# Forgetting attention with a channel mix on one core: the first two heads' bias summed in place, a 1e-9 added by another engine, and first sums of values put into a transpose bank

## The chip, the cores and the metric

The kernel is one program on one core of a Trainium2 chip. The metric is the device time of one execution in microseconds (us), taken as the median of several runs. Engines are named as in the profile: PE (matmul) with PEld (its weight load), DVE (vector), ACT (scalar), POOL (GpSimd) and SP, which issues every DMA of this kernel from one queue.

## The reference

Eight batches of eight heads with 576 positions and 64 features go through attention with a forgetting bias; the result, laid out as 512 features, goes through a gated channel mix.

```python
scores = (q @ k.T) / sqrt(D)
cum = cumsum(maximum(s, 0), axis=-1)
bias = -(cum[:, :, :, None] - cum[:, :, None, :])
scores = where(causal, -1e9, scores + minimum(bias, 0))
attn = exp(scores - max(scores))
attn = attn / (sum(attn) + 1e-9)
x = (attn @ v)                       # (batch, seq, 512)
x_prev = x one position earlier
xk = mu_k * x + (1 - mu_k) * x_prev
xr = mu_r * x + (1 - mu_r) * x_prev
out = sigmoid(xr @ w_r) * (maximum(xk @ w_k, 0) ** 2 @ w_v)
```

## The kernel before, in words

Every instruction is first a task in a list (`Plan.add`): its engine, an estimated duration, what it reads and writes, and a due time. `Plan.run` then plays the list forward through a model of the engines, computes new due times backward from what came out, and repeats that `PASSES` times; the order with the shortest modelled time is written out. So an engine executes its instructions in an order fixed by the estimates, and waits at the head of its queue if reality is later. The estimates belong to the edits: `dve` and `pool` give an instruction its modelled duration, and `dma` gives a transfer `land=700` ns after its issue, to which the model adds 1,000 ns after any DMA and 30 to 500 ns before its user. While PE has nothing planned at the start, the planner writes small matmuls into its queue (line 359) until the first product of weights and values, `plan.busy_from`.

The attention runs head by head in "visits" of two heads (`hp`), batch after batch. Batch 0 is visited in two parts: queries 0 to 319 (`A`, 320 keys) for all four pairs, then queries 320 to 575 (`Z`). The other seven batches are visited whole (`ALL`). That is 72 passes through `scores`: 8 of `A`, 8 of `Z`, 56 of `ALL`. The first eight visits (16 heads' passes) use values and weights in plain float32 (`plain`), the others split them in a high and a low part.

`scores` for one head: a row of prefix sums of `s` is read from DRAM (`cum_d`) broadcast on all 128 partitions as `CB` (tag `cb`, two buffers, line 605). POOL makes the causal copy `M` of its blocks at the diagonal (tag `mask`, two buffers, line 624). PE multiplies queries and keys into a PSUM bank (line 642 plain, 653 split), DVE adds the bias and keeps the row's extreme value (line 668), ACT takes the exponent and the row's sum (line 686, into `sums`), DVE adds 1e-9 (line 723) and takes the reciprocal (line 728, into `rinv`), and POOL multiplies the weights `W` by it (line 699).

The prefix sums come from `prefix_sums`: `s` of all 64 heads lands on 64 partitions (line 419), DVE clips and scales it (424) and scans it (431), and a DMA stores it to `cum_d` (437). Its two buffers have the tag `cb` too.

`weighted` for one head: PE transposes the normalized weights block by block into PSUM banks with the tag `t` (line 745; two such banks, taken in turn), ACT copies a block to `ph` (772, 804), DVE takes what `ph` lost into `pl` (776, 811). In an `ALL` pass four banks are filled so: the last one holds the blocks of keys 256 to 383 in columns 0 to 255, and of keys 384 to 511 in columns 256 to 383. Then PE multiplies by the values (line 861 plain, 877 split): the sums of queries 0 to 127 go into a fifth bank of the tag `t`, those of queries 128 to 575 into the bank `po`. ACT (898 plain, 905) and DVE (909) take them to `xT`, which is stored to `x_d` (line 1202).

The channel mix works on 18 chunks of 256 positions: `x` is loaded from `x_d` (line 1104), mixed (951, 960) and split (979, 983), PE does three matmul passes for each weight block (1012, 1054, 1079), and `g` is stored (1096). The weights arrive in float64 words and are converted once by ACT, DVE and POOL (lines 483 to 514). POOL also makes the low parts of keys (`KL`, line 582), queries (`G`, 593) and values (`V`, 538), for each head.

Of the kernel before, what the change touches and what calls it, by code (L numbers as in the profile page):

```python
# [15 lines left out]
AF = mybir.ActivationFunctionType  # L16
# [37 lines left out]
class Plan:  # L54
# [210 lines left out]
        return [-x for x in at]  # L265


    PASSES = 4

    def run(self):  # L270
        best = None
# [14 lines left out]
def forgetting_attention_then_channel_mix(  # L286
# [38 lines left out]
    def sbuf(shape, tag, bufs=1, dtype=F32):  # L325
        return plan.buffer(sb, shape, dtype, tag, bufs)

    def bank(n, tag, bufs=1):
        return plan.buffer(psum, [P, 512 * n], F32, tag, bufs)
# [7 lines left out]
    def pe(emit, reads, writes, n, m=P, cycle=1.0625 / 2.4, k=P):  # L337
        i = plan.add("PE", n * cycle, emit, reads, writes, land=0.83 * m + 1)
        plan.columns[i] = n * k / P * (4 if cycle > 1 else 1)
        return i  # L340

    def act(emit, reads, writes, n, extra=51, table=0):
        return plan.add("ACT", n * 0.8333 + extra, emit, reads, writes, land=table)

    def dve(emit, reads, writes, n, rate=0.96):
        return plan.add("DVE", n / rate + 68, emit, reads, writes)

    def pool(emit, reads, writes, n, extra, rate=0.8333):
        return plan.add("POOL", n * rate + extra, emit, reads, writes)

    def dma(emit, reads, writes, ns):
        return plan.add("SP", max(520, ns), emit, reads, writes, land=700)


    idle = bank(1, "po", 1)
# [56 lines left out]
    cum_d = fixed(dram.tile([B * H, S], F32, name="cum_d"))  # L412

    def prefix_sums():
        cum = sbuf([B * H, S], "cb", 2)
        spos = sbuf([B * H, S], "cb", 2)
        ones = sbuf([B * H, S], "raw", 4)
        dma(
            lambda: nc.sync.dma_start(spos.get(), s.rearrange("b h t -> (b h) t")),
            [], [spos], 410,  # L420
        )
        pool(lambda: nc.gpsimd.memset(ones.get(), 1.0), [], [ones], S, 36)
        dve(
            lambda: nc.vector.tensor_scalar(
                out=spos.get(), in0=spos.get(), scalar1=0.0, scalar2=ISCALE,
                op0=ALU.max, op1=ALU.mult,
            ),
            [], [spos], S,
        )
        dve(  # L430
            lambda: nc.vector.tensor_tensor_scan(
                out=cum.get(), data0=ones.get(), data1=spos.get(), initial=0.0,
                op0=ALU.mult, op1=ALU.add,
            ),
            [ones, spos], [cum], 2 * S,
        )
        dma(lambda: nc.sync.dma_start(cum_d.ap, cum.get()), [cum], [cum_d], 410)


    def load_mu():  # L440
# [78 lines left out]


    ALL, A, Z = tuple(range(NQ)), (0, 1, 2), (3, 4)

    def load_values(b, hp, nk, plain):

# [75 lines left out]
    def scores(b, h, tiles, G, KH, KL):  # L600

        NK = KN[tiles[-1]]
        CB = sbuf([P, NK], "cb", 2)
        dma(
            lambda: nc.sync.dma_start(
                CB.get(), cum_d.ap[b * H + h : b * H + h + 1, 0:NK].broadcast_to([P, NK])
            ),
# [108 lines left out]
        for t in tiles:  # L716
            m, n, W = QN[t], KN[t], pt[t]
            i = 0
            for k0, w in [(0, n)] if n <= 512 else [(0, n // 2), (n // 2, n // 2)]:
                i = products(t, m, i, k0, w, W)  # L720
            exponents(t, m, n, i - 1, W)
        dve(
            lambda: nc.vector.tensor_scalar(  # L723
                out=rs(rinv), in0=rs(sums), scalar1=1.0e-9, scalar2=None, op0=ALU.add
            ),
            [(sums, t) for t in tiles], [rinv], len(tiles),
        )
        dve(lambda: nc.vector.reciprocal(rs(rinv), rs(rinv)), [], [rinv], 8 * len(tiles))  # L728
        for t in tiles:
# [3 lines left out]
    def weighted(j, pt, V, xT, tiles, plain):  # L733
# [17 lines left out]
        def block(ps, at, kb, n=1):  # L751

            ts = [t for t in tiles if t > kb]
            q0, q1 = QS[ts[0]], QS[ts[-1]] + P
            m = q1 - q0
            for k in range(kb, kb + n):
                for t in ts:
                    turn(ps, at + (k - kb) * m + QS[t] - q0, t, k * P, P)

            def strips(x):  # L760
                a = col(kb, q0)
                if n == 1:
                    return x.get()[:, a : a + m]
                step = col(kb + 1, q0) - a
                return x.get()[:, a : a + n * step].rearrange("p (k x) -> p k x", x=step)[:, :, 0:m]

            def src():
                x = ps.get()[:, at : at + n * m]
                return x if n == 1 else x.rearrange("p (k x) -> p k x", x=m)

            ks = range(kb, kb + n)
            act(lambda: nc.scalar.copy(strips(ph), src()), [ps], [(ph, k) for k in ks], n * m)  # L772
            if plain:
                return
            dve(
                lambda: nc.vector.tensor_tensor(  # L776
                    out=strips(pl), in0=src(), in1=f32(strips(ph)), op=ALU.subtract
                ),
                [ps] + [(ph, k) for k in ks], [(pl, k) for k in ks], n * m,
            )  # L780
# [47 lines left out]
        if len(tiles) == NQ:  # L828
            ps = bank(1, "t", 2)
            halves(ps, 0, 1, NQ - 1)  # L830
            ps = bank(1, "t", 2)
            block(ps, 0, 0)
            ps = bank(1, "t", 2)
            halves(ps, 384, 0, 0)
            block(ps, 0, 1)
            ps = bank(1, "t", 2)
            block(ps, 0, 2)
            block(ps, 256, 3)
        elif tiles[0] == 0:
            ps = bank(1, "t", 2)  # L840
            halves(ps, 256, 0, 0)
            block(ps, 0, 0)
            ps = bank(1, "t", 2)
            halves(ps, 0, 1, 2)
            block(ps, 256, 1)
        else:
            ps = bank(1, "t", 2)
            block(ps, 0, 0, 2)
            ps = bank(1, "t", 2)
            block(ps, 0, 2)  # L850
            ps = bank(1, "t", 2)
            halves(ps, 0, 3, 4)
            block(ps, 256, 3)
        lo, ot = 64 * j, 64 * (1 - j)

        def values(po, base, kb, q0, m, x, first, last):
            parts = [("h", kb), "l" if kb == NQ - 1 else kb]
            if plain:
                r = slice(0, 64 if kb == NQ - 1 else P)
                i = pe(  # L860
                    lambda: nc.tensor.matmul(
                        po.get()[:, q0 - base : q0 - base + m],
                        V.get()[r, kb],
                        x.get()[r, col(kb, q0) : col(kb, q0) + m],
                        start=first,
                        stop=last,
                    ),
                    [V] + [(x, i) for i in parts[: 2 if kb < NQ - 1 else 1]],
                    [po], m, P, 4 / 2.4, r.stop,
                )  # L870
                if plan.busy_from is None:
                    plan.busy_from = i
                return

            both = x is ph or last
            pe(
                lambda: nc.tensor.matmul(  # L877
                    po.get()[: P if both else 64, q0 - base : q0 - base + m],
                    V.get()[:, kb, 2 * j : 2 * j + (2 if both else 1), :],
                    x.get()[:, col(kb, q0) : col(kb, q0) + m],  # L880
                    start=first,
                    stop=last,
                ),
                [(V, i) for i in range(3)] + [(x, i) for i in parts], [po], m, P if both else 64,
            )

        def sums(po, q0, q1):

            todo = []
            for kb in range(-(-q1 // P)):  # L890
                a = max(q0, kb * P)
                todo += [(kb, a, x) for x in ((ph, pl) if kb < NQ - 1 and not plain else (ph,))]
            for i, (kb, a, x) in enumerate(todo):
                values(po, q0, kb, a, q1 - a, x, i == 0, i == len(todo) - 1)
            n = q1 - q0
            if plain:
                act(
                    lambda: nc.scalar.copy(
                        xT.get()[lo : lo + 64, 1 + q0 : 1 + q1], po.get()[lo : lo + 64, :n]
                    ),  # L900
                    [po], [(xT, (j, q0))], n,
                )
                return
            act(
                lambda: nc.scalar.copy(xT.get()[lo : lo + 64, 1 + q0 : 1 + q1], po.get()[ot : ot + 64, :n]),
                [po], [(xT, (j, q0))], n,
            )
            dve(
                lambda: nc.vector.tensor_tensor(  # L909
                    out=xT.get()[lo : lo + 64, 1 + q0 : 1 + q1],  # L910
                    in0=po.get()[lo : lo + 64, :n],
                    in1=xT.get()[lo : lo + 64, 1 + q0 : 1 + q1],
                    op=ALU.add,
                ),
                [po], [(xT, (j, q0))], n,
            )

        for q0, q1 in sums_of(tiles):
            sums(bank(1, "t", 2) if q1 == P else bank(1, "po", 1), q0, q1)

    def sums_of(tiles):

# [234 lines left out]
        due += 2 * STEPS[x]  # L1157

    plan.due = -2.0e5
    prefix_sums()  # L1160
    QKs, Vs = {}, {}

# [115 lines left out]
```

## Time and profile before

| | |
|---|---|
| median of 3 runs | 927.6 us (923.38 to 927.82) |
| the profiled execution | 925.86 us, its span 923.9 us, 2.0 us lie outside the span |
| mean granted PE clock | 0.978 |
| busy shares of the span | PE 95%, PEld 81%, DVE 76%, ACT 74%, POOL 51% |
| DMA | 109.56 MB, mean 119 GB/s |

Busy time is the union of an engine's instructions. PE's matmuls are pipelined and their ends are modelled, so its share is an upper limit of its work. The first 100 us differ from the rest: the weights are loaded and converted there, 243 GB/s move, and the granted PE clock is lower.

### The profile page before, as it was taken

How to read it: one execution, taken by the hardware profiler on the slowest of the kernel's cores; microseconds unless marked ns; L12 is line 12 of the kernel's file. 1: busy time of each engine (PE TensorE's matmuls, PEld its weight loads, DVE VectorE, ACT ScalarE, POOL GpSimd, SP SyncE). 2: the span in 40 equal slices, each digit the busy share in tenths (PEclk: the TensorE clock that was granted, in tenths of full speed). 3: DMA queues.
4: the chain of work that ended last, by engine and by line, in shares of the span. 5: the costliest groups of instructions: out<-in, count | busy, mean ns of one | idle time of the engine just before them, and what ended most of it. 6: DMA issues, size and time to landing. Idle time of an engine off the chain costs nothing.

```text
span 923.9 us, 18424 instructions
## 1 busy us (share of the span) xinstructions
PE 882.2 (95%) x5540; PEld 751.4 (81%) x5540; DVE 701.7 (76%) x2455; ACT 683.1 (74%) x1809; POOL 474.0 (51%) x783
## 2 busy tenths in 40 slices
PE   6979899999999999999999999999999999999998
PEld 3558777877879798978888988888888879888886
DVE  7956889989987888678878787878787878545431
ACT  4868798989987888688868697878786867445331
POOL 4876697787774476555546654555564641100000
PEclk7779999999999999999999999999999999999999
DMA  7878545455452344434243533343434220101100
GB/s 255 256 224 234 150 148 151 131 155 152 123 168 91 110 130 117 120 108 143 90 137 105 151 104 115 95 132 99 144 103 126 79 85 15 41 31 36 46 23 23
DMA packets 63651, 109.56 MB, mean 119 GB/s; under 512 B 10176, under 2 KB 25024, under 8 KB 63552
## 3 DMA queue, kind: packets, MB, share of 16 engines
q1 hardware_dynamic: 63552, 108.40, 39.4%
q8 instruction: 43, 0.70, 0.3%
q14 instruction: 56, 0.46, 0.2%
HBM read 89.33 MB, written 19.04 MB: 117 GB/s over the span
## 4 chain that ended last, share of the span: by engine, by line
PE 33%; DVE 10%; ACT 7%; issue 2%; DMA 2%; POOL 0%; DVEq 0%; ACTq 0%; POOLq 0%
PE m L1012 12%; PE m L1079 8%; PE m L1054 5%; PE t L745 3%; PE po L877 3%; DVE W L668 3%; PE s L653 2%; DVE xp L960 2%; ACT xp L951 2%; ACT W L686 2%; DVE rinv L723 1%; DVE pl L776 1%; DMA x<-x_d 1%; DVE xT L909 1%; ACT ph L772 1%
## 5 line engine op out<-in xcount | busy, mean ns | idle before, releaser
L1012 PE MATMUL m<-xh,w_k 128*128 128x256 f32 x1152 | 232.6, 288 | 2.2 <-DVE kl L1041 2.1
L686 ACT ACTIVATE W<-W,nm 64x64 f32<-64x64 f32 (+4 forms) x320 | 179.7, 562 | 37.7 <-DVE nm L668 31.8
L745 PE MATMUL t<-ident,W 128*128 128x128 f32 (+1 forms) x960 | 191.4, 281 | 14.7 <-DVE pl L776 6.5
L1079 PE MATMUL m<-w_v,kh 128*128 128x512 f32 x576 | 201.3, 406 | 0.0
L1012 PEld LDWEIGHTS m<-xh,w_k 128*128 128x128 f32 x1152 | 186.2, 190 | 4.9 <-DVE kl L1041 2.9
L699 POOL TENSOR_SCALAR W<-W,rinv 64x64 f32<-64x64 f32 (+4 forms) x320 | 163.8, 531 | 42.7 <-DVE rinv L728 29.9
L1012 PE MATMUL m<-xl,w_k 128*128 128x256 f32 x576 | 165.1, 287 | 0.2
L745 PEld LDWEIGHTS t<-ident,W 128*128 128x128 f32 (+1 forms) x960 | 114.0, 132 | 53.3 <-DVE pl L776 13.8
L582 POOL TENSOR_TENSOR KL<-raw,KH 128x576 fp32r<-128x576 f32 x64 | 92.1, 1438 | 110.7 <-ACT KH L578 101.0
L1079 PEld LDWEIGHTS m<-w_v,kh 128*128 128x128 f32 x576 | 107.2, 189 | 18.0 <-ACT g L1066 0.2
L653 PE MATMUL s<-KH,G 128*64 128x64 f32 (+3 forms) x360 | 112.9, 321 | 4.5 <-DVE nm L668 3.9
L1079 PE MATMUL m<-w_v,kl 128*128 128x512 f32 x288 | 116.6, 405 | 0.0
L960 DVE SCALAR_TENSOR_TENSOR xp<-x,mu,xp 128x256 f32<-128x256 f32 (+3 forms) x192 | 80.6, 420 | 47.3 <-ACT xp L951 44.7
L668 DVE CUSTOM_DVE_ANT_0 W<-s,cb 128x64 f32<-128x64 f32 (+3 forms) x256 | 94.5, 374 | 26.4 <-PE s L653 19.3
L776 DVE TENSOR_TENSOR pl<-t,ph 128x512 fp32r<-128x512 f32 x224 | 105.2, 481 | 10.1 <-ACT ph L772 8.8
L1012 PEld LDWEIGHTS m<-xl,w_k 128*128 128x128 f32 x576 | 109.4, 190 | 1.7 <-DVE xl L983 0.9
L653 PE MATMUL s<-KL,G 128*64 128x64 f32 (+3 forms) x360 | 108.8, 304 | 0.0
L772 ACT CAST ph<-t 128x512 fp32r<-128x512 f32 x224 | 92.8, 421 | 17.0 <-PE t L745 15.8
L951 ACT ACTIVATE xp<-x,mu 128x256 f32<-128x256 f32 (+3 forms) x192 | 81.3, 424 | 31.4 <-DMA x<-x_d 9.7
L1054 PE MATMUL m<-w_r,xh 128*128 128x512 f32 x288 | 102.4, 408 | 1.5 <-DVE kl L1041 1.5
L593 POOL TENSOR_TENSOR G<-raw,G 64x576 fp32r<-64x576 f32 (+1 forms) x64 | 85.7, 1338 | 25.7 <-issue 13.6
L877 PE MATMUL po<-ph,V 128*128 128x448 f32 x280 | 91.8, 334 | 0.3 <-ACT ph L772 0.3
(101 smaller groups left out, 1762.2 us busy)
## 6 DMA issues: line engine op xcount, KB each, us to landing
raw<-in_k SPq DMA_DIRECT2D x128, 144.0 KB, 3.3
cb<-cum_d SPq DMA_DIRECT2D x64, 288.0 KB, 3.7
raw<-in_q SPq DMA_DIRECT2D x112, 144.0 KB, 3.3
out<-g SPq DMA_DIRECT2D x36, 256.0 KB, 2.4
vn<-in_v SPq DMA_DIRECT2D x28, 320.0 KB, 3.3
x_d<-xT SPq DMA_DIRECT2D x28, 288.5 KB, 2.5
x<-x_d SPq DMA_DIRECT2D x12, 514.0 KB, 4.0
w_k<-in_moe_w_k SPq DMA_DIRECT2D x8, 512.0 KB, 5.6
```

What stands on the lines that cost most here:

```text
L653: lambda x=x, K=K: nc.tensor.matmul(ps.get()[:m, :w], G.get()[:, q0 : q0 + m], K.get()[:, k0 : k0 + w], start=x == 0, stop=x == 1,),
L668: lambda a=a, e=e, bias=bias, i=i: nc.vector.tensor_tensor_reduce(out=W.ap[:m, a:e], in0=ps.get()[:m, a - k0 : e - k0], in1=bias.get()[:m, ...
L686: lambda: nc.scalar.activation(W.ap[:m, :n], W.ap[:m, :n], AF.Exp, bias=nm.get()[:m, 3 * t + mi : 3 * t + mi + 1], scale=-1.0, accum_out=s ...
L699: lambda: nc.gpsimd.tensor_scalar(out=W.ap[:m, :n], in0=W.ap[:m, :n], scalar1=rinv.get()[:m, t : t + 1], scalar2=1.0, op0=ALU.mult, op1=AL ...
L745: lambda: nc.tensor.transpose(ps.get()[0:m, place : place + P], pt[t].ap[:, k0 : k0 + m], ident.ap),
L772: act(lambda: nc.scalar.copy(strips(ph), src()), [ps], [(ph, k) for k in ks], n * m)
L776: lambda: nc.vector.tensor_tensor(out=strips(pl), in0=src(), in1=f32(strips(ph)), op=ALU.subtract),
L877: lambda: nc.tensor.matmul(po.get()[: P if both else 64, q0 - base : q0 - base + m], V.get()[:, kb, 2 * j : 2 * j + (2 if both else 1), :] ...
L951: lambda n=n, o=o, i=i, to=to: nc.scalar.activation(to(), x.get()[:, c, o + i + 1 : o + i + 1 + n], AF.Copy, scale=mu.ap[:, which, c : c + 1],
L1012: lambda u=u, f=f, c=c, n=n, w=w, x=x: nc.tensor.matmul(ps.get()[:, u * CT : (u + 1) * CT], weight["k", c, f // 4].get()[:, w, f % 4 * P : ...
L1054: lambda c=c, n=n, x=x, w=w: nc.tensor.matmul(ps.get(), x.get()[:, c, ts], weight["r", c, 0].get()[:, w], start=c == 0 and n == 0, stop=c ...
L1079: lambda f=f, n=n, x=x, w=w: nc.tensor.matmul(ps.get(), x.get()[:, f, ts], weight["v", f, 0].get()[:, w], start=f == 0 and n == 0, stop=f ...
```

## The change

Six edits are made together. (1) `first_sums` is new: for the first two heads of batch 0, keys 0 to 319, `s` is loaded broadcast on all 128 partitions, ACT clips and scales it, and two DVE scans write the prefix sums straight into the two `cb` buffers, so that the first two passes have no load of `CB`. (2) The buffers of `prefix_sums` move from the tag `cb` to the tag `mask`. (3) The 1e-9 of line 723 is added by POOL. (4) In an `ALL` pass, the sums of queries 0 to 127 go into columns 384 to 511 of the fourth transpose bank, and no fifth bank is taken. (5) The planner's `dma` has `land=1300` for 700. (6) `PASSES` is 8 for 4. `plan.busy_from` can now also be set by a split product; the plain ones come first.

```diff
-    PASSES = 4
+    PASSES = 8
...
-        return plan.add("SP", max(520, ns), emit, reads, writes, land=700)
+        return plan.add("SP", max(520, ns), emit, reads, writes, land=1300)
...
     def prefix_sums():
-        cum = sbuf([B * H, S], "cb", 2)
-        spos = sbuf([B * H, S], "cb", 2)
+        cum = sbuf([B * H, S], "mask", 2)
+        spos = sbuf([B * H, S], "mask", 2)
...
+    def first_sums(nk):
+
+        raw = sbuf([P, 2, nk], "raw", 4)
+        ones = sbuf([P, nk], "raw", 4)
+        cbs = [sbuf([P, nk], "cb", 2) for _ in range(2)]
+        dma(
+            lambda: nc.sync.dma_start(raw.get(), s[0:1, 0:2, 0:nk].broadcast_to([P, 2, nk])),
+            [], [raw], 819 * 2 * nk / S,
+        )
+        pool(lambda: nc.gpsimd.memset(ones.get(), 1.0), [], [ones], nk, 36)
+        act(
+            lambda: nc.scalar.activation(raw.get(), raw.get(), AF.Relu, scale=ISCALE),
+            [], [raw], 2 * nk, 94,
+        )
+        for j in range(2):
+            dve(
+                lambda j=j: nc.vector.tensor_tensor_scan(
+                    out=cbs[j].get(), data0=ones.get(), data1=raw.get()[:, j], initial=0.0,
+                    op0=ALU.mult, op1=ALU.add,
+                ),
+                [ones, raw], [cbs[j]], 2 * nk,
+            )
+        return cbs
...
-        CB = sbuf([P, NK], "cb", 2)
-        dma(
+        CB = sbuf([P, NK], "cb", 2) if not first else first.pop(0)
+        (b == 0 and h < 2 and tiles == A) or dma(
...
-        dve(
-            lambda: nc.vector.tensor_scalar(
+        pool(
+            lambda: nc.gpsimd.tensor_scalar(
                 out=rs(rinv), in0=rs(sums), scalar1=1.0e-9, scalar2=None, op0=ALU.add
             ),
-            [(sums, t) for t in tiles], [rinv], len(tiles),
+            [(sums, t) for t in tiles], [rinv], len(tiles), 100,
         )
...
             block(ps, 0, 2)
             block(ps, 256, 3)
+            rest = ps
...
-                po.get()[:, q0 - base : q0 - base + m],
+                po.get()[:, at + q0 - base : at + q0 - base + m],
...
         for q0, q1 in sums_of(tiles):
-            sums(bank(1, "t", 2) if q1 == P else bank(1, "po", 1), q0, q1)
+            sums(*((rest, 384) if q1 == P else (bank(1, "po", 1), 0)), q0, q1)
...
     plan.due = -2.0e5
+    first.extend(first_sums(KN[A[-1]]))
     prefix_sums()
```

## Rows read from the trace of the kernel before

**Rows 1.** The page: span, and busy time of each engine

```profile
span 923.9 us, 18424 instructions
...
PE 882.2 (95%) x5540; PEld 751.4 (81%) x5540; DVE 701.7 (76%) x2455; ACT 683.1 (74%) x1809; POOL 474.0 (51%) x783
```

**Rows 2.** Windows by stage: stretch, its length, busy us (instructions), clock, DMA share, GB/s

```profile
0.00:100.00 100.00, 85.15 (x411) 59.85 (x412) 74.24 (x248) 71.70 (x200) 62.21 (x121) 0.81 0.81 243
...
424.00:770.00 346.00, 339.96 (x2261) 298.50 (x2260) 279.57 (x1010) 271.33 (x722) 188.98 (x308) 1.00 0.37 112
770.00:924.00 154.00, 147.39 (x867) 128.51 (x865) 72.98 (x158) 64.53 (x141) 5.13 (x10) 0.99 0.09 32
```

**Rows 3.** Chain that ended last, 424 to 800 us: shares by line; start, us, what

```profile
by line: PE m L1012 17.9%; PE m L1079 10.0%; PE t L745 7.0%; DVE W L668 6.2%; PE m L1054 6.1%; PE po L877 6.1%; PE s L653 6.0%; issue 5.1%; ACT W L686 3.8%; DVE xp L960 3.0%; DVE rinv L723 2.7%; ACT xp L951 2.7%; DVE pl L776 2.4%; DMA x<-x_
...
436.67 0.62 DVE rinv L723
...
654.70 4.22 DMA x<-x_d
...
759.13 0.17 DVE rinv L723
```

**Rows 4.** Line 723: durations in ns (min/median/max); DVE busy on it by stretch

```profile
L723 DVE TENSOR_SCALAR rinv<-sums x72: 148/263/2742, 18.4 to 786.8; 128x5 f32<-128x5 f32 x56, 128x3 f32<-128x3 f32 x8, 128x2 f32<-128x2 f32 x8
...
0.00:100.00 100.00, 6.17 (x14) 0.81 0.81 243
100.00:424.00 324.00, 14.35 (x29) 1.00 0.44 129
424.00:800.00 376.00, 16.39 (x29) 1.00 0.35 105
```

**Rows 5.** Timeline at 667 us: start, us, engine and line, what, [idle before, releaser]

```profile
667.22 1.42 POOL L593 TENSOR_TENSOR G<-raw,G 64x576 fp32r<-64x576 f32 x1
667.27 1.40 DVE L723 TENSOR_SCALAR rinv<-sums 128x5 f32<-128x5 f32 x1 [0.35 <-ACT W L686]
```

**Rows 6.** Timeline at 51 to 55 us, DVE and ACT

```profile
51.57 2.74 DVE L723 TENSOR_SCALAR rinv<-sums 128x3 f32<-128x3 f32 x1 [0.17 <-ACT W L686]
...
54.99 0.62 ACT L512 CAST w_r<-xl 128x512 fp32r<-128x512 f32 x1 [3.45 <-DVE rinv L728]
```

**Rows 7.** Timeline of the first 15 us

```profile
0.73 0.57 SPq L419 DMA_DIRECT2D cb<-in_s  x1
...
4.22 1.35 DVE L431 TENSOR_TENSOR_SCAN cb<-raw,cb 64x576 f32<-64x576 f32 x1
...
5.60 0.48 SPq L437 DMA_DIRECT2D cum_d<-cb  x1
...
13.18 0.59 POOL L624 TENSOR_SCALAR_AFFINE_SELECT mask<-cb 64x64 f32<-64x64 f32 x2 [1.57 <-DMA cb<-cum_d]
...
14.28 1.83 PE L642 MATMUL s<-KH,G 64*128 64x320 f32 x4 [5.51 <-DVE nm L668]
```

**Rows 8.** Windows of the opening: busy PE, PEld, DVE, ACT, POOL, then PE clock

```profile
12.00:36.00 24.00, 21.72 (x64) 12.13 (x65) 21.01 (x78) 17.30 (x54) 16.07 (x34) 0.52 0.87 278
36.00:60.00 24.00, 18.22 (x65) 10.83 (x66) 19.23 (x65) 16.24 (x53) 17.84 (x32) 0.71 0.71 219
```

**Rows 9.** Groups of POOL: busy us, mean ns, idle before and releasers

```profile
L582 POOL TENSOR_TENSOR KL<-raw,KH 128x576 fp32r<-128x576 f32 x64 | 92.1, 1438 | 110.7 <-ACT KH L578 101.0 <-ACT ph L804 8.7 <-DMA raw<-in_k 0.2
...
L699 POOL TENSOR_SCALAR W<-W,rinv 64x64 f32<-64x64 f32 x64 | 20.0, 312 | 2.8 <-DVE rinv L728 2.8
...
L612 POOL MEMSET sums<- 128x1 f32 x64 | 6.0, 95 | 28.1 <-DVE rinv L723 24.3 <-DMA cb<-cum_d 2.3 <-DVE pl L811 0.3
```

**Rows 10.** Waits: who waited for whom, us in total, times, longest

```profile
POOL KL L582 <- ACT KH L578: 101.0, 30, 8.4
...
ACT xT L905 <- PE t L877: 11.0, 16, 1.5
...
PE t L745 <- DVE pl L776: 6.5, 13, 0.9
```

More of the change, by code (lines that the diff above doesn't have):

```diff
@@ L521, in forgetting_attention_then_channel_mix @@
     ALL, A, Z = tuple(range(NQ)), (0, 1, 2), (3, 4)
+    first = []
     def load_values(b, hp, nk, plain):
@@ L854, in weighted, with values @@
         lo, ot = 64 * j, 64 * (1 - j)
-        def values(po, base, kb, q0, m, x, first, last):
+        def values(po, base, at, kb, q0, m, x, first, last):
             parts = [("h", kb), "l" if kb == NQ - 1 else kb]
@@ L875, in values @@
             both = x is ph or last
-            pe(
+            i = pe(
                 lambda: nc.tensor.matmul(
-                    po.get()[: P if both else 64, q0 - base : q0 - base + m],
+                    po.get()[: P if both else 64, at + q0 - base : at + q0 - base + m],
                     V.get()[:, kb, 2 * j : 2 * j + (2 if both else 1), :],
@@ L885, in values, with sums @@
             )
-        def sums(po, q0, q1):
+            if plan.busy_from is None:
+                plan.busy_from = i
+        def sums(po, at, q0, q1):
             todo = []
@@ L893, in sums @@
             for i, (kb, a, x) in enumerate(todo):
-                values(po, q0, kb, a, q1 - a, x, i == 0, i == len(todo) - 1)
+                values(po, q0, at, kb, a, q1 - a, x, i == 0, i == len(todo) - 1)
             n = q1 - q0
@@ L898, in sums @@
                     lambda: nc.scalar.copy(
-                        xT.get()[lo : lo + 64, 1 + q0 : 1 + q1], po.get()[lo : lo + 64, :n]
+                        xT.get()[lo : lo + 64, 1 + q0 : 1 + q1], po.get()[lo : lo + 64, at : at + n]
                     ),
@@ L904, in sums @@
             act(
-                lambda: nc.scalar.copy(xT.get()[lo : lo + 64, 1 + q0 : 1 + q1], po.get()[ot : ot + 64, :n]),
+                lambda: nc.scalar.copy(xT.get()[lo : lo + 64, 1 + q0 : 1 + q1], po.get()[ot : ot + 64, at : at + n]),
                 [po], [(xT, (j, q0))], n,
@@ L910, in sums @@
                     out=xT.get()[lo : lo + 64, 1 + q0 : 1 + q1],
-                    in0=po.get()[lo : lo + 64, :n],
+                    in0=po.get()[lo : lo + 64, at : at + n],
                     in1=xT.get()[lo : lo + 64, 1 + q0 : 1 + q1],
```

## The prediction, made before the changed kernel was run

> **What bounds the kernel now.** I read the page first, then the windows by stage, the chain, and last the lines that the change touches. PE is busy for 882.2 of 923.9 us [rows 1], and from 770 us on for 147.4 of 154 [rows 2]: the tail is nearly all matmul of the channel mix, and none of the six edits touches it. Between 424 and 770 us PE is busy for 340 of 346 us [rows 2], which seems to leave 6 us; but those ends are modelled, and the chain tells more. Of its 376 us from 424 to 800 us, the PE lines shown carry 53% (17.9 + 10.0 + 7.0 + 6.1 + 6.1 + 6.0), the rest are steps of DVE, ACT, issue and DMA [rows 3]. So that stage is a list of four engines' queues that wait for each other, and a late vector instruction does cost. The first 100 us are another matter: PE is busy for 85, the clock is at a mean of 0.81, DMA is busy for 0.81 at 243 GB/s [rows 2]; between 12 and 60 us DVE has 40.2 of 48 us [rows 8].
>
> **The 1e-9 (edit 3).** This is the edit with a visible price. Line 723 works on five numbers a partition and takes 148 ns at best, 263 in the median, 2,742 at most [rows 4]. Its 72 instructions take 6.17 + 14.35 + 16.39 = 36.9 us; at 0.16 us each (estimated from the minimum) they would take 11.5, so 25.4 us are stall. What they stall on is seen at 667 us: POOL starts a subtraction at 667.22 for 1.42 us, DVE starts line 723 at 667.27, and both end within 0.03 us (668.64 and 668.67) [rows 5]. At 51.57 one takes 2.74 us and ACT idles 3.45 us behind it [rows 6].
>
> The Trainium skill states why (SBUF — State Buffer, section "Who interferes with whom"): the ports that VectorE and GpSimd share are an exclusive lock for a whole instruction, and a VectorE tensor_scalar between SBUF tensors can take it, while whoever starts first holds the other off. The times at 667 us agree. By that rule an add on POOL cannot collide with POOL's own subtraction, so the stall leaves DVE entirely; were the 1.40 us the cost of the operation itself, it would move along and this term would be nothing.
>
> How much of the 25.4 us is on the path? On the chain from 424 us, line 723 has 2.7% of 376 us, 10.2 us, in ten pieces from 436.67 to 759.13 [rows 3]; less 1.6 for ten unblocked ones, 8.6 of the 11.8 us of stall in that stretch (16.39 - 29 x 0.16), or 73%. The same share of the 9.7 us between 100 and 424 is 7.1, and 2.6 us are that one at 51.57: 18 us at most. Nothing at least, if parallel paths are as late: DVE, ACT and PE hand a chain to each other in pieces of half a microsecond, so a path that is 1 us shorter soon meets its neighbour. I take a third, **-6**.
>
> The add itself has no row on POOL. Nearest are a memset of one column, 95 ns, and a tensor_scalar of 64 columns, 312 ns [rows 9]. Against 0.16 on DVE that is -0.07 to +0.15 us for each of 72, -5 to +11 us were all on the path. Closer is the tensor_scalar, as an operation; a third of the heads' adds stand in the chain (10 of 29), so +3.6 at that end, -1.6 at the other; **+1**. It gains POOL a little: the memset of line 612 waits 24.3 us for DVE's line 723 [rows 9], and that wait falls away. POOL has half its span free. What is queued behind: on POOL the normalization (699) waits for the reciprocal as before; on DVE the reciprocal (728) now waits for POOL, and behind it everything that DVE has in order.
>
> **The first two heads (edits 1, 2).** Now: `s` is asked for at 0.73, the scan runs from 4.22 for 1.35 us, the store is issued at 5.60, and the mask starts at 13.18, after the broadcast load; PE idles 5.51 us before 14.28 [rows 7]. Store and load are 7.6 us of chain. Afterwards the bias of head 0 needs the broadcast load (as late as the present one, some 3.7), one ACT step over 640 elements and a scan of 320 (0.75 us from 1.35 for 576): around 6 us. But the first mask goes into the buffer that the store reads, so it starts when the store has finished, and the load alone is saved. If the 7.6 us divide about evenly between the two transfers, that is near 9.4, plus up to 1.5 us if the new scans go ahead of the old one: 2.3 to 3.8 us saved for head 0. Two scans are 1.5 us more on DVE; ACT gets about 0.6; the added DMA carries what the two dropped loads carried. DMA is busy for 0.87 of 12 to 36 us [rows 8], and weights that land no sooner may swallow the gain. Bounds 0 and -5.5 (the idle PE time); I take **-2.5**. A granted clock of 0.52 over 12 to 36 us [rows 8] means that PE ran almost wholly at 1.2 GHz there, after its 5.5 us of idleness; a shorter gap may keep 2.4 GHz longer. DVE's idle time of 7.8 us in 12 to 60 bounds what that is worth; I count nothing for it here, and it goes to a rival.
>
> **The bank (edit 4).** Five fillings of `t` become four in each of 56 passes. Transposes wait 6.5 us for DVE to empty a bank, and ACT waits 11.0 us for the small products that had the fifth one [rows 10]. On the other side, those products must now wait for the evictions of the fourth bank. The large products need those evictions too, so the small ones lose only their head start. Bounds +2 and -3, **0**.
>
> **The planner (edits 5, 6).** No instruction is added. With 1,300 ns a load of 256 positions of `x` is modelled at 1,459 (5.7 ns each in the code) + 1,300 + 1,000 ns and the gap before its user, near 4 us, where the chain has one of 4.22 [rows 3]; 700 was short. Better order is likelier than worse, but any reordering of 18,000 instructions moves waits about; +5 to -5, **-1**.
>
> Sum: 925.9 - 6 + 1 - 2.5 - 1 = 917.4 against the profiled execution. The median of the runs lies 1.7 higher; I say **918**.
>
> **Rivals.** *The stall was cover* (no change): other engines were as late as DVE, the start is held by the weights' transfers, and 925.9 + 1 - 1 gives 926. For it: PE busy for 340 of 346 us [rows 2]. Against it: the share of line 723 in the chain. On the same side stands a rule of the Trainium skill (GPSIMD Engine Reference, section "Engine selection"): elementwise work belongs on VectorE. By it the add would have gained nothing by moving, and only the start would be left; no unblocked add of POOL is in this trace to weigh it. Chance 0.18.
>
> *The wait changes sides* (slower): POOL executes in order. Line 582 waits for ACT 30 times, 101 us in all, 3.4 us each [rows 10]. Where the planner puts such a subtraction ahead of the add and ACT is late, DVE stands at the reciprocal for those 3.4 us. At the same weight as above (6 of 25.4, 0.24), the kernel becomes slower once these waits pass 25.4 + 2.5 / 0.24 = 36 us, some eleven heads. With 18 heads, 61 us, it takes 925.9 + 0.24 x 36 - 2.5 = 932; with 30, 942. Against it: a late ACT also delays the sums themselves, so the add is seldom ready earlier. Chance 0.12, around 936.
>
> *More than I count* (faster still): two thirds of the stall are on the path (-12), and the shorter first gap keeps PE at its higher clock, of DVE's 7.8 us of idle time 5 go: 925.9 - 12 - 5 + 1 - 1 = 909. For it: the 73% of the chain. Against it: DVE at 0.88 of 12 to 36 us. Chance 0.15.
>
> **Numbers.** My own case has 0.55, from 911 to 923. With the faster rival that is 0.70 for faster by over 0.5% (4.6 us, about what a measurement of this kernel can tell from no change), 0.18 for the same, 0.12 for slower. The range 907 to 931 leaves out half of the faster rival (0.07) and the slower one (0.12).
>
> **What would show it.** DVE has no line 723, and its busy time falls by some 33 us, 36.9 less the two scans and what reordering does; on POOL the add takes 0.1 to 0.3 us; idle time of DVE before the reciprocal stays under 10 us in all. If it is over 36, the slower rival has it. The first mask starts before 11 us and PE's gap before its second batch of products shrinks from 5.5 to 2 or 3 us. The stretch at half clock becomes shorter if the faster rival is right. Transposes wait less for DVE. The tail from the last attention pass to the end keeps its length, near 137 us (from 787). I am wrong if the chain after has the same length with ACT or PE where line 723 stood.

## The result and the profile after

The changed kernel takes 914.46 us (median of 4 runs, 912.39 to 916.06) against 926.61 us for the kernel before: 12.2 us less, a ratio of 0.9863 with a 95% interval of 0.9833 to 0.9894. The profiled execution took 912.39 us with a span of 910.6 us.

The page of the changed kernel, span and busy time, answers to [rows 1]:

```profile
span 910.6 us, 18389 instructions
...
PE 885.3 (97%) x5539; PEld 758.9 (83%) x5539; DVE 672.3 (74%) x2385; ACT 682.1 (75%) x1810; POOL 494.5 (54%) x856
```

DVE has lost 29.4 us of busy time (some 33 were forecast) and POOL gained 20.5. PE is busy for 3 us more in a span that is 13.3 us shorter. The chain of [rows 3] is followed back from the end of the run, before to 424 us, in the changed kernel only to 517 us. So the two are compared here from 520 to 800 us, shares by line, the kernel before first; line 748 is the add now, 753 the reciprocal:

```profile
by line: PE m L1012 18.6%; PE m L1079 8.9%; PE t L745 7.1%; PE m L1054 6.2%; PE po L877 6.0%; DVE W L668 6.0%; PE s L653 5.6%; issue 4.9%; ACT W L686 3.5%; DVE xp L960 3.3%; DMA x<-x_d 3.1%; DVE rinv L723 2.9%; ACT xp L951 2.7%; DVE xT L909
```

```profile
by line: PE m L1040 25.0%; PE m L1107 13.1%; PE t L770 8.7%; PE s L678 8.3%; PE m L1082 8.2%; PE po L903 7.8%; DVE W L693 3.8%; ACT xp L979 2.7%; ACT W L711 2.7%; issue 2.6%; DVE xp L988 2.3%; POOL W L724 2.0%; DMA cb<-cum_d 1.7%; DVE xT L9
```

The add, 2.9% of that stretch before, is not among the lines shown any more; the vector line that leads, the bias (668, now 693), falls from 6.0 to 3.8%, the exponent on ACT from 3.5 to 2.7%. The PE lines shown rise from 52 to 71%: the chain is PE's own work for more of its length. The add on POOL and the reciprocal on DVE, durations in ns (min/median/max), and what ended DVE's idle time before the reciprocal:

```profile
L748 POOL TENSOR_SCALAR rinv<-sums x72: 227/238/251, 13.9 to 774.1; 128x5 f32<-128x5 f32 x56, 128x3 f32<-128x3 f32 x8, 128x2 f32<-128x2 f32 x8
```

```profile
L753 DVE RECIPROCAL rinv<-rinv x72: 155/182/195, 14.7 to 774.4; 128x5 f32<-128x5 f32 x56, 128x3 f32<-128x3 f32 x8, 128x2 f32<-128x2 f32 x8
its engine sat idle before it (us, times) until:
  POOL rinv L748: 15.7, 21
```

Where VectorE spent 36.9 us in line 723, GpSimd spends 17.1 (72 x 0.238) and VectorE waits 15.7 us at the reciprocal.

The opening of the changed kernel in the timeline answers to [rows 7]:

```profile
1.35 0.57 SPq L445 DMA_DIRECT2D raw<-in_s  x1
...
5.54 0.48 SPq L437 DMA_DIRECT2D cum_d<-mask  x1
5.86 0.74 ACT L450 ACTIVATE raw<-raw 128x640 f32<-128x640 f32 x1 [3.86 <-DMA raw<-in_s]
6.70 1.54 DVE L455 TENSOR_TENSOR_SCAN cb<-raw,raw 128x320 f32<-128x320 f32 x2 [1.18 <-ACT raw L450]
...
8.31 0.59 POOL L649 TENSOR_SCALAR_AFFINE_SELECT mask<-cb 64x64 f32<-64x64 f32 x2 [3.76 <-DVE cb L455]
...
9.79 0.60 POOL L649 TENSOR_SCALAR_AFFINE_SELECT mask<-cb 64x64 f32<-64x64 f32 x2 [0.89 <-DMA cum_d<-mask]
...
11.05 0.80 PE L667 MATMUL s<-KH,G 64*128 64x320 f32 x2 [2.16 <-DVE nm L693]
```

One head's mask starts at 8.31, the one that needs the stored buffer at 9.79, after the store, and PE's gap before its next batch of products is 2.16 us instead of 5.51. Windows of the opening (busy PE, PEld, DVE, ACT, POOL, then the clock) answer to [rows 8]:

```profile
12.00:36.00 24.00, 23.57 (x71) 13.22 (x71) 21.71 (x81) 18.75 (x61) 17.93 (x39) 0.53 0.92 279
36.00:60.00 24.00, 22.39 (x84) 14.55 (x83) 18.64 (x64) 19.07 (x59) 20.16 (x35) 0.68 0.75 222
```

The granted clock, 0.53 and 0.68, is no higher than before (0.52 and 0.71) [rows 8]: the time at 1.2 GHz is no shorter.

### The profile page after: what moved, and what is told of

Same layout as the page of the kernel before. It is cut to its first block, busy times and chain, and to the rows that moved or that the text cites. A ratio compares the mean times of both kernels' runs of the same rounds, so it can differ in the third digit from the quotient of the medians.

```text
span 910.6 us, 18389 instructions
## 1 busy us (share of the span) xinstructions
PE 885.3 (97%) x5539; PEld 758.9 (83%) x5539; DVE 672.3 (74%) x2385; ACT 682.1 (75%) x1810; POOL 494.5 (54%) x856
## 5 line engine op out<-in xcount | busy, mean ns | idle before, releaser
L770 PE MATMUL t<-ident,W 128*128 128x128 f32 (+1 forms) x960 | 185.7, 281 | 6.0 <-ACT ph L797 1.4
L1107 PEld LDWEIGHTS m<-w_v,kh 128*128 128x128 f32 x576 | 106.1, 189 | 19.1 <-POOL w_v L538 0.7
L678 PE MATMUL s<-KL,G 128*64 128x64 f32 (+2 forms) x360 | 107.6, 300 | 0.0
L693 DVE CUSTOM_DVE_ANT_0 W<-s,mask,nm 128x128 f32<-128x128 f32 x256 | 87.3, 344 | 4.9 <-PE t L770 0.4
```

The costliest lines, as they stand in the source:

```text
L678: lambda x=x, K=K: nc.tensor.matmul(ps.get()[:m, :w], G.get()[:, q0 : q0 + m], K.get()[:, k0 : k0 + w], start=x == 0, stop=x == 1,),
L693: lambda a=a, e=e, bias=bias, i=i: nc.vector.tensor_tensor_reduce(out=W.ap[:m, a:e], in0=ps.get()[:m, a - k0 : e - k0], in1=bias.get()[:m, ...
L770: lambda: nc.tensor.transpose(ps.get()[0:m, place : place + P], pt[t].ap[:, k0 : k0 + m], ident.ap),
L1107: lambda f=f, n=n, x=x, w=w: nc.tensor.matmul(ps.get(), x.get()[:, f, ts], weight["v", f, 0].get()[:, w], start=f == 0 and n == 0, stop=f ...
```

## The experiments

Every kernel but the change itself was timed in five rounds beside the kernel before on the same chip; ratios are to that kernel. Any edit that the planner sees gives a new order on all engines. Four runs (the three with "order" in their names and u_bank_none) therefore keep an order and change only what one task issues; the others are planned anew, and a few us of theirs can be luck. The changed kernel without edit 3, planned anew, was not run, nor was edit 5 alone. Where line 723's work goes, "lost VectorE time" is the time in the add plus the waits at the reciprocal.

| run | what | ratio (95% interval) |
|---|---|---|
| the change | all six edits | 0.9863 (0.9833 to 0.9894) |
| b_order_reduce | before, same order, line 723 in a form without the stall | 0.9869 (0.9844 to 0.9893) |
| b_order_pool | before, same order, add on GpSimd | 1.0083 (1.0061 to 1.0105) |
| a_order_dve | changed, same order, add on VectorE | 0.9875 (0.9852 to 0.9899) |
| a_pool | before with edit 3 alone | 0.9913 (0.9885 to 0.9941) |
| a_first | before with edits 1, 2 alone | 0.9996 (0.9979 to 1.0012) |
| a_bank | before with edit 4 alone | 1.0024 (1.0009 to 1.0039) |
| u_first | changed without edits 1, 2 | 0.9866 (0.9847 to 0.9886) |
| u_bank | changed without edit 4 | 0.9747 (0.9726 to 0.9768) |
| u_land | changed without edit 5 | 0.9904 (0.9887 to 0.9921) |
| u_pass | changed without edit 6 | 0.9832 (0.9814 to 0.9850) |
| a_noadd | changed, no add, planned anew | 0.9879 (0.9862 to 0.9896) |
| u_bank_none | u_bank in its order, no add | 0.9776 (0.9762 to 0.9791) |

**The stall by itself (b_order_reduce).**

```diff
         dve(
-            lambda: nc.vector.tensor_scalar(
-                out=rs(rinv), in0=rs(sums), scalar1=1.0e-9, scalar2=None, op0=ALU.add
-            ),
+            lambda: nc.vector.tensor_reduce(
+                out=rs(rinv), in_=rs(sums).rearrange("p (t x) -> p t x", x=1),
+                axis=mybir.AxisListType.X, op=ALU.add,
+            ),
```

> The kernel before in its own order, instruction for instruction; only line 723 changes its form: VectorE takes a sum over one element (a reduction) instead of adding 1e-9, so the 1e-9 is left out. Theory 'lock' (the 25.4 us of stall come from ports that a VectorE tensor_scalar and GpSimd exclude each other from, and about a third of it lies on the path): the line takes 0.15 to 0.25 us each time, never over 0.4, and the kernel takes 4 to 9 us less than before, 918 to 923. Rival 'cover' (the stall happens but other engines were as late): the line is short too, but the time stays within 2 us of before. Rival 'cost' (small vector instructions are slow there whatever their form): the line keeps a mean near 0.5 us and the time stays.

Line 723 of this run, durations in ns:

```profile
L723 DVE TENSOR_REDUCE rinv<-sums x72: 141/156/164, 18.2 to 777.5; 128x5 f32<-128x5 f32 x56, 128x3 f32<-128x3 f32 x8, 128x2 f32<-128x2 f32 x8
```

The same five numbers, at the same place behind the same neighbours, take 164 ns at most where they took up to 2,742 [rows 4]: the rival "cost" is out. The same is seen by counting in the timelines. In the kernel before, all 41 adds of over 220 ns started while an instruction of POOL was running and ended within 60 ns of the end of one, and the 24 that started while POOL was idle took 172 ns at most; in this run 49 started while POOL was running, and none was held. The order is the old one, and the time falls by 1.31%, 12.1 us of 926.6, more than the 4 to 9 that I expected, so "cover" is out as well. The line takes 11.1 us in all instead of 36.9; of 25.8 us taken away, 12.1 arrive at the end, nearly half. The Trainium skill (SBUF — State Buffer, section "Who interferes with whom") says of reductions on this chip that they never contend for the shared ports; these 72 agree.

**The same add on GpSimd, the order unchanged (b_order_pool).**

```diff
-            lambda: nc.vector.tensor_scalar(
+            lambda: nc.gpsimd.tensor_scalar(
                 out=rs(rinv), in0=rs(sums), scalar1=1.0e-9, scalar2=None, op0=ALU.add
```

> The kernel before in its own order, with the add of 1e-9 issued by GpSimd at the same place of the order. Theory 'lock': the add takes 0.1 to 0.3 us on GpSimd, VectorE's reciprocal waits under 10 us in all, and the kernel takes 3 to 8 us less than before. Rival 'the wait changes sides': the planner did not place the add for GpSimd here, so it stands behind subtractions, VectorE waits over 20 us at the reciprocal, and the time is that of before or longer. Rival 'cover': the time stays within 2 us.

Waits of this run, VectorE's two longest (us in total, times, longest):

```profile
DVE xp L960 <- ACT xp L951: 49.5, 66, 5.0
DVE rinv L728 <- POOL rinv L723: 48.4, 47, 3.0
```

This is the slower rival in the flesh. The add takes 0.238 us as in the changed kernel, but it stands in POOL's queue where the planner believed POOL to be doing other things, and VectorE waits 48.4 us for it. Lost VectorE time goes from 36.9 to 48.4 us, and the kernel is 0.83% slower, 7.7 us. POOL is held at the add too, 41.0 us until ACT's exponents are there; this run does not separate the two. So the add's being on another engine does not pay by itself.

**The same add on VectorE in the new order (a_order_dve).**

```diff
-            lambda: nc.gpsimd.tensor_scalar(
+            lambda: nc.vector.tensor_scalar(
                 out=rs(rinv), in0=rs(sums), scalar1=1.0e-9, scalar2=None, op0=ALU.add
```

> The changed kernel in its own order, with the add of 1e-9 issued by VectorE at the same place of the order. Theory 'lock': the line takes 0.4 to 0.6 us in the mean, with pieces of over 1 us, and the kernel takes 4 to 9 us more than the changed one, 918 to 924. Rival 'order' (the 12 us come from the planner's new order, the start and the bank): it stays within 2 us of the changed kernel, near 914 to 916.

```profile
L748 DVE TENSOR_SCALAR rinv<-sums x72: 148/166/1379, 14.1 to 776.1; 128x5 f32<-128x5 f32 x56, 128x3 f32<-128x3 f32 x8, 128x2 f32<-128x2 f32 x8
```

```profile
0.00:100.00 100.00, 4.69 (x14) 0.81 0.83 249
100.00:424.00 324.00, 10.46 (x30) 1.00 0.46 132
424.00:800.00 376.00, 6.09 (x28) 1.00 0.35 101
```

My expectation missed, and the rival "order" stands: the time is that of the changed kernel within the intervals. The two views (durations of line 748; VectorE's busy time on it by stretch) say why. In this order the same tensor_scalar takes 21.2 us in all, median 166 ns: only 9.7 us of stall are left (21.2 - 72 x 0.16). Only 24 of the 72 adds start while POOL is running, where it was 48 in the kernel before. The memset that clears the next pass's sums on POOL shows what POOL does instead:

```profile
L637 POOL MEMSET sums<- x64: 91/98/103, 2.8 to 746.9; 128x1 f32 x64
...
  DVE rinv L748: 63.0, 38
```

In 38 cases, 63.0 us in all, POOL stands at this memset and waits for VectorE's add; in the kernel before it was 24.3 us [rows 9]. So most of the stall goes because the order has POOL standing still at the add, whichever engine executes it.

**Edit 3 alone, planned (a_pool).** The diff is the add's of the change.

> The kernel before with edit 3 alone (the 1e-9 added by GpSimd), planned anew. By the four runs so far, VectorE time that is lost at line 723 or at the reciprocal behind it costs about half of itself at the end (25.8 us less gave 13.2, 11.5 more cost 7.0). Theory 'planned wait' (a planner that knows where the add runs places it so that VectorE waits for it about as little as in the changed kernel, 15 to 20 us instead of 36.9): 8 to 11 us less than before, 916 to 919. Rival 'the other edits made room' (the short wait of the changed kernel needs its new order): VectorE waits 30 to 48 us and the time is that of before or up to 7 us more.

```profile
DVE rinv L728 <- POOL rinv L723: 21.8, 28, 2.5
```

That wait, in VectorE's list, is under half of the 48.4 us of the unplanned version, and the kernel is 0.87% faster, 8.1 us: two thirds of the whole gain. "The other edits made room" is out, though the changed kernel waits 6 us less.

Whether the gain inside the bundle is the same one is not shown. The first reciprocal of the first whole visit, the seventeenth of 72, shows how far each kernel is by then (before, changed, a_pool, b_order_reduce; one execution each):

```profile
128.50 0.18 DVE L728 RECIPROCAL rinv<-rinv 128x5 f32<-128x5 f32 x1
```

```profile
119.01 0.19 DVE L753 RECIPROCAL rinv<-rinv 128x5 f32<-128x5 f32 x1 [0.36 <-POOL rinv L748]
```

```profile
126.61 0.19 DVE L728 RECIPROCAL rinv<-rinv 128x5 f32<-128x5 f32 x1 [1.23 <-POOL rinv L723]
```

```profile
126.54 0.18 DVE L729 RECIPROCAL rinv<-rinv 128x5 f32<-128x5 f32 x1
```

The changed kernel is 9.5 us ahead there, of 13.3 at the end of its span; edit 3 alone is 1.9 ahead, of 5.5, and the form without the stall 2.0, of 9.3. So most of the bundle's lead arises in the opening, where edit 3 alone brings little. No single edit that was taken out removes it (u_first is 7.4 us ahead at that place, u_bank 6.8, u_land 10.0, u_pass 8.3), and an early lead need not reach the end: a_bank is 5.4 ahead there and behind at the end.

**The start (a_first, u_first).** The diffs are edits 1 and 2, done alone and undone.

> The kernel before with edits 1 and 2 alone (first two heads' bias summed in place, the prefix sums in the mask's buffers), planned anew. Theory 'start': the first weights' products come 3 us earlier and 2.5 us of it are kept at the end, 922 to 925. Rival 'swallowed': transfers of the first 60 us take it back, and the time is within 1 us of before. Rival 'more': the earlier start also spares PE time at half clock, 5 us or more.

> The changed kernel without edits 1 and 2 (the first two heads load their bias from DRAM again), planned anew. Theory 'start swallowed', from the run of these edits alone: within 2 us of the changed kernel, 913 to 917. Rival 'start kept': 2.5 to 4 us more, 917 to 919. A new order can move either by a few us.

The add in a_first, with the first and last start at the end of the first part:

```profile
L749 DVE TENSOR_SCALAR rinv<-sums x72: 152/238/1409, 15.7 to 788.7; 128x5 f32<-128x5 f32 x56, 128x3 f32<-128x3 f32 x8, 128x2 f32<-128x2 f32 x8
```

The first add comes 2.7 us earlier than before (15.7 against 18.4), the last one 1.9 us later (788.7 against 786.8) [rows 4]. Alone, and taken out of the changed kernel, these two edits are worth nothing that can be measured. Both "swallowed" readings hold in the time. But it is not the weights' transfers of the opening that swallow the gain: a_first's seventeenth reciprocal still comes 2.7 us earlier than the 128.50 of the kernel before, long after its own last weights landed (at 101 us),

```profile
125.78 0.19 DVE L754 RECIPROCAL rinv<-rinv 128x5 f32<-128x5 f32 x1
```

and the lead is gone only after 590 us. What takes it there stays open.

**The bank (u_bank, a_bank).** The diff undone, or done alone:

```diff
-            sums(*((rest, 384) if q1 == P else (bank(1, "po", 1), 0)), q0, q1)
+            sums(bank(1, "t", 2) if q1 == P else bank(1, "po", 1), q0, q1)
```

> The changed kernel without edit 4 (the first sums of values take a fifth transpose bank again), planned anew. Theory 'bank neutral': within 2 us of the changed kernel, 913 to 917, PE's and its weight load's waits for banks go up by some 10 us without moving the end. Rival 'bank pays': 3 us or more above it, 918 or more.

> The kernel before with edit 4 alone (first sums of values in the free columns of the fourth transpose bank), planned anew. Theory 'bank costs' (the small products wait for the last evictions, and the next pass's second bank waits for their copies, so that ACT and VectorE wait more): 5 us or more above the kernel before, ratio 1.005 to 1.012. Rival 'luck of the order' (the 10 us gained without this edit came from another plan, not from the bank): ratio 0.996 to 1.004.

Without the bank edit the kernel is another 1.2% faster, some 10.7 us (0.9863 - 0.9747), and the edit alone makes the kernel before slower by 0.24%. Waits of the changed kernel, then of u_bank:

```profile
ACT xT L933 <- PE t L903: 16.9, 20, 1.9
...
DVE xT L937 <- ACT xT L933: 13.9, 15, 1.8
...
PEld t L770 <- DVE pl L801: 5.3, 16, 0.8
```

```profile
ACT xT L930 <- PE t L902: 12.7, 14, 1.5
...
DVE xT L934 <- ACT xT L930: 11.3, 20, 1.0
...
PEld t L770 <- DVE pl L801: 7.1, 16, 0.8
```

Between these two the reasons of the prediction are there: transposes wait less for a bank (5.3 against 7.1 us), ACT and VectorE wait longer for the small products and their copies (30.8 against 24.0). But 7 us of waits are not 10.7 us at the end, and other plans moved the changed kernel by -3 to +4 us without touching the bank. u_bank lies outside both of its forecasts. a_bank lies inside its rival "luck of the order" (0.996 to 1.004), and its ACT and VectorE do not wait longer for the small products (18.7 us against 19.1 before). So that the bank costs is not shown; how much of the 10.7 us is the bank's and how much the plan's stays open. No run here holds the order and changes the bank alone: that was not tried.

**The planner (u_land, u_pass).**

```diff
-        return plan.add("SP", max(520, ns), emit, reads, writes, land=1300)
+        return plan.add("SP", max(520, ns), emit, reads, writes, land=700)
```

```diff
-    PASSES = 8
+    PASSES = 4
```

> The changed kernel with the planner's landing time of 700 ns again (edit 5 undone), planned anew. Theory 'landing neutral': a ratio to the kernel before of 0.984 to 0.990, as for the changed kernel. Rival 'landing pays' (a truer estimate keeps engines from waiting at the head of their queues for DMAs): 0.991 or more, with more waits for DMAs.

> The changed kernel with 4 passes of the planner (edit 6 undone): another order comes out, while on the kernel before 8 passes give the same order as 4. Theory 'a better plan' (later passes are truly better): ratio to the kernel before 0.988 to 0.995. Rival 'a lottery': anywhere from 0.975 to 0.995, and as likely below the changed kernel's 0.986 as above.

With 700 ns the ratio is 0.0041 higher, some 4 us, between the two forecasts; the intervals overlap, and other plans moved the kernel as far. ACT's wait for loads of `x`, first in the changed kernel, then in u_land:

```profile
ACT xp L979 <- DMA x<-x_d: 8.0, 9, 3.3
```

```profile
ACT xp L979 <- DMA x<-x_d: 19.3, 9, 3.8
```

Nine waits in both, but 11.3 us more in all. Over all traces here ACT waits 9.7 to 19.4 us for these loads with 700 ns (9.7 in the kernel before) and 6.0 to 12.2 with 1,300: the truer estimate goes with shorter waits, and that it is worth 4 us is not shown. Four passes instead of eight give 0.9832, no slower than eight; and on the kernel before, 8 passes and 4 write out the same order. More passes bought nothing here.

**No add at all (a_noadd, u_bank_none).** In u_bank_none the place of the add stays in the plan and issues nothing:

```diff
-            lambda: nc.gpsimd.tensor_scalar(
-                out=rs(rinv), in0=rs(sums), scalar1=1.0e-9, scalar2=None, op0=ALU.add
-            ),
+            lambda: None,
...
-        dve(lambda: nc.vector.reciprocal(rs(rinv), rs(rinv)), [], [rinv], 8 * len(tiles))
+        dve(lambda: nc.vector.reciprocal(rs(rinv), rs(sums)), [], [rinv], 8 * len(tiles))
```

> The changed kernel, planned anew, with the add of 1e-9 left out: the reciprocal reads the sums. Every sum holds an exponent of 0, so it is at least 1, and 1e-9 is lost in rounding at that size. If half of VectorE's 15.7 us of waiting at the reciprocal is on the path: 5 to 8 us less than the changed kernel, 906 to 909. Rival 'nothing left': other engines take over, within 2 us of 914.5.

> The changed kernel without edit 4, in the order of that run, instruction for instruction; the add of 1e-9 is left out and the reciprocal reads the sums (each is at least 1, so 1e-9 is lost in rounding). Theory 'half price' (VectorE time lost at this place costs half of itself): VectorE loses its 15.8 us of waiting for GpSimd, and the kernel takes 6 to 9 us less than that run, a ratio of 0.965 to 0.969 to the kernel before. Rival 'nothing left' (what the run with a new plan and no add suggested: another engine is as late): within 2 us of that run, a ratio of 0.973 to 0.977.

In u_bank_none the sums' buffer is released at the place of the add, so a reciprocal can read sums that a later pass has begun to write; the instructions and their sizes are those of u_bank. The reciprocal there, and what ended the idle time before it:

```profile
L751 DVE RECIPROCAL rinv<-sums x72: 159/179/193, 15.9 to 768.2; 128x5 f32<-128x5 f32 x56, 128x3 f32<-128x3 f32 x8, 128x2 f32<-128x2 f32 x8
...
  ACT W L711: 3.1, 4
  POOL sums L637: 2.0, 6
  ACT ph L827: 1.0, 1
```

VectorE's wait falls from 15.8 us in u_bank to 6.1, and nothing is gained (0.9776 against 0.9747; the intervals just meet). POOL's wait only moves: 49.5 us at the add for ACT's exponents in u_bank, and here 65.8 us at the weights (line 724) for the reciprocal, a wait of 8.1 us in u_bank. With a new plan and no add the kernel is no faster than with it. So my "half price" falls: 25.8 us of stall in an order that did not know of it cost half; some ten us of waiting in an order that was planned around it cost nothing. That the planner had filled the other engines around that wait is a reading of this, not shown.

u_bank, the change without its bank edit, is the fastest of all: 904.69 us, 23.8 below the kernel before on its chip.

## Why the prediction was right, step by step

The time (914.5 for 918) lies in the range and in my own case, 911 to 923. Edit 3 alone gives the largest gain of the edits that were tried alone, as forecast; that it gives as much inside the bundle is not shown. The terms of the sum were off, and that their errors offset each other is luck.

- **The stall, taken at -6.** The mechanism is right as far as it can be seen: VectorE is held while an instruction of POOL runs, and the form of b_order_reduce is not. That it is ports that hold it is the reason that the prediction gives; no run looks at them. The size was too small. I took a third of a possible 18 us, 6; in the old order the whole stall is worth 12.1, halfway between the two.
- **The add on POOL, taken at +1.** Its duration, 0.238 us, is between my two rows. Its wait was to stay under 10 us and is 15.7. Leaving most of such a wait out gained nothing measurable in u_bank's order (u_bank_none). Edit 3 as a whole, alone and planned, gave -8.1 against my -5.
- **The wait that changes sides.** It did not come in the changed kernel, whose order is planned for the add. Unplanned, it came at 48.4 us, past my threshold of 36, and the kernel was slower; at my price of 0.24 a microsecond that is 0.24 x (48.4 - 25.4) = 5.5 us, and 7.7 were measured.
- **The first two heads, taken at -2.5.** The places are right (first masks at 8.31 and 9.79, PE's gap from 5.51 to 2.16 us), the end gets nothing. The bound "nothing" that I gave was the answer, but not for my reason: the lead outlasts the weights' transfers.
- **The bank, taken at 0.** Between the changed kernel and u_bank both waits moved the way I said; in a_bank ACT's did not. Done alone it costs 2.2 us, undoing it gains 10.7, outside my +2, with the plan's share of that unknown.
- **The planner, taken at -1.** Undoing the landing time costs about 4 us, inside my bounds and no more than another plan can move; the passes bring nothing.
- **More than I count** had PE at its higher clock for longer. That did not happen: 0.53 and 0.68 in the changed kernel's windows. In a_first's profiled execution it did (0.61 and 0.78), and the end gained nothing. The tail kept its length, 136 us after the last reciprocal at 774.4.

## What to carry to other kernels

A tiny instruction with a small minimum and a large maximum is worth a look at what another engine does at the same time: here the stall of 72 adds on two to five numbers cost 12 us, and a form that the other engine does not hold off brought as much as the whole change. In a kernel whose order is planned, the planner must know where a moved instruction runs: here the same move gave +7.7 us unplanned and -8.1 planned. Test each edit of a bundle both alone and taken out, the main one too, and keep the order fixed where you can; one of six here may have held the others back.

## What was not expected of the hardware

An instruction that another engine holds off can be held by several of its instructions in turn. The longest case in the kernel before, VectorE's add of 2.74 us from 51.57 to 54.31 [rows 6], spans three GpSimd instructions in its timeline:

```profile
51.43 0.40 POOL L624 TENSOR_SCALAR_AFFINE_SELECT mask<-cb 128x256 f32<-128x256 f32 x1
...
51.80 1.26 POOL L514 TENSOR_TENSOR w_r<-xl,w_r 128x512 fp32r<-128x512 f32 x1
...
53.03 1.26 POOL L514 TENSOR_TENSOR w_r<-xh,w_r 128x512 fp32r<-128x512 f32 x1
```

They follow each other without a gap and end at 54.29; the add ends 0.02 us later. The Trainium skill's section named above tells of one instruction that blocks another; that a queue of them can keep VectorE out from one to the next rests on this case and one shorter: the add at 21.73 us takes 0.54 us, through the last 0.16 us of one instruction of POOL and the 0.40 us of the next, and ends 0.03 us after it.
